# Sink-window attention with a softplus layer on one Trainium2 core: values of the first two chunks as 128 zero-padded columns, and 136 score columns for a batch's first query block

## The chip, the core and the metric

The kernel runs on one core of a Trainium2 chip. The metric is the device time of one launch, in microseconds (us). Before the change three runs took 724.26, 724.29 and 725.24 us, with a median of 724.29 us.

## What is computed

```python
def _attn_ref(q, k, v, n_sink, window):          # 4 batches, 8 heads, 768 positions, 64 per head
    scores = scale * np.matmul(q, k.transpose(0, 1, 3, 2))
    is_sink = pos[None, :] < int(n_sink)         # n_sink = 4
    rel = pos[:, None] - pos[None, :]
    in_window = (rel >= 0) & (rel < int(window)) # window = 128
    scores = np.where(is_sink | in_window, scores, -1000000000.0)
    a = np.exp(scores - np.max(scores, axis=-1, keepdims=True))
    a = a / (np.sum(a, axis=-1, keepdims=True) + 1e-09)
    return np.matmul(a, v)
...
def _moe_ref(x, w_in, w_out):                    # 3072 tokens, 512 -> 2048 -> 512
    h = x @ w_in
    g = np.maximum(h, 0.0) + np.log1p(np.exp(-np.abs(h)))
    return g @ w_out
```

A query sees itself, the 127 positions before it and the first four positions of its batch (the sinks). What the heads give is put side by side, 512 values a token, and goes through the two-layer part.

## The kernel before

The 3072 tokens are cut into 12 chunks of 256 (`CT`), three a batch, and a chunk into two query blocks of 128 (`CH = 2`, index j). Chunks 0, 3, 6 and 9 are the first of their batch (`first`, with `i0 == 0`). Heads are numbered on through all chunks below, so that V11 is `values` of head 3 of chunk 1, T24 is `softmax` of head 0 of chunk 3, and so on.

For a head, `scores` (S) multiplies a query block with 264 columns of keys: the block of keys ahead of it and 8 sink keys (136 columns, `KW`), and then its own block of keys (128 columns). A query sees some keys of both blocks, and for a given place in a block exactly one of two. So `softmax` (T) lays both on each other: `copy_predicated` (L258, on VectorE) puts the scores of the own block over those of the block ahead, where the mask `diag` says so, and a custom reduction (L264) works on the 136 columns that are left, then ScalarE's exp (L265). In a batch's first block (j = 0 of chunks 0, 3, 6 and 9) there is no block ahead, and the layout of the keys puts the own block there a second time.

`normalise` (N) divides; `weights_t` (W) transposes the 128 columns with TensorE (tile `t`), copies them (`th`, and `tl`, the rest that the rounding of `th` leaves) and has GpSimd unfold them into `pt`, with zeros where the other block of keys would stand. `sink_weights` and `sink` (k, K) do the like with the 8 sink columns of four heads at once (`sa`, `ts`, `sk`). `values` (V) is then one product of the sinks' values with `sk` (L342) and two or three products of blocks of values with `pt` (L348), all added in PSUM in the tile `x`, of which there is one. `out` (O) splits `x` into the rounded `xh` and the rest `xl`.

The products have two forms. Chunks 0 and 1 are `exact`: their operands are plain float32, and the profile counts each product as two instructions on TensorE (transposes as one). Later chunks split each number into a float32r high part and a low part and add up products of those; each is one instruction. In `exact` chunks the keys and queries of two heads come together (tiles `k` and `q`, from arrays that the host has laid out, with zeros in q in the half of the other head). The values are loaded for two heads, and a head's 64 columns are its stationary operand: an even head writes partitions 0 to 63 of `x`, an odd one 64 to 127.

The two-layer part of a chunk runs one chunk later: `up` (U, tile `h`, L474), `softplus` and `gate` (F, P, tiles `mt`, `gh`), `residue` (R, `gl`), `down` (D and E, tile `acc`, L511 to L513). Its weights come as 64-bit words in 32 pieces of 512 KB (tiles `wi00r` to `wo71r`, L383), and VectorE, ScalarE and GpSimd turn each into a high and a low float32r part (tiles `upper`, `wt` or `word_ps`, then `wi` or `wo`) while chunks 0 and 1 are worked on.

TensorE and the DMA queue of SyncE run in the order in which the program is written: for chunks 0 and 1 a list of steps by hand (`START`), and from then on two alternating strings of step letters. The other engines' order is set by a scheduler that simulates the program. In `START`, L is `load`, G is `load_v`, w loads a piece of weights, and a, c, d, l are its conversion:

```python
Ctx.START = """
j4 w w w J0 S0 T0 G4 w S1 S2 w N0 L8 T1 T2 S3 w N1 L10 S4 W1 T3 a N2 W0 w T4 a N3 S5 k0 c c K0 a S6
w d c T5 d V0 V1 l N4 l W2 T6 w d O0 a G6 c S7 W3 O1 l N5 N6 T7 z18 V2 a a c N7 d W4 k4 S8 a T8 O2 w V3
...
```

`L10` loads keys and queries into the tiles that S6 and S7 read, so SyncE's queue stands still at it until S7 is done, with the pieces of weights `wi20r` and the rest behind it. The values of chunk 0's heads 4 to 7 and of chunk 1 are loaded at G4, G6, G8, G10, G12 and G14.

Of the kernel before, what the change touches and what calls it, by code (L numbers as in the profile page):

```python
# [11 lines left out]
F32 = mybir.dt.float32  # L12
# [8 lines left out]
B, H, S, D = 4, 8, 768, 64  # L21
DM, DFF = 512, 2048
P = 128
NB = S // P
NS = 8
KW = P + NS
CH = 2
# [10 lines left out]
G = 4  # L38
# [84 lines left out]
class _Attention:  # L123
# [86 lines left out]

    def load_v(self, g):
        c, nc, chunk, lo = self.c, self.c.nc, self.chunk, self.vlo
        tag, bufs = ("kl" if chunk == 0 and g > 1 else "vv", 2) if self.exact else ("vr", 1)
        vr = c.lp.tile([P, 3, 2 * D], F32, tag=tag, name=f"vr{chunk}_{g}", bufs=bufs)
        rows = slice(self.i0 - 1 + lo, self.i0 + 2)
        nc.sync.dma_start(
            vr[:, lo:], c.a["v"][self.b, rows, :, g * 2 * D : (g + 1) * 2 * D].rearrange("n p d -> p n d")
        )
        self.v[g] = vr

    def split_v(self, g):
# [7 lines left out]
        _sub(nc, c.E["vl"], vv[:, lo:, :, 1], src, vv[:, lo:, :, 0])  # L229
        self.v[g] = vv  # L230

    def scores(self, h):
        c, nc = self.c, self.c.nc
        ops = self.heads.pop(h)
        for j in range(CH):
            pool, tag = (c.ps_h, "h") if self.chunk == 0 and h % 2 else (c.ps_s, "s")
            s = pool.tile([P, 2 * P + NS], F32, tag=tag, name=f"s{self.chunk}_{h}_{j}")
            mv = slice(j * KW, j * KW + 2 * P + NS)
            st = slice(KC + j * P, KC + j * P + P)
            if self.exact:  # L240
                q, k = ops
                nc.tensor.matmul(s[:], q[:, j * P : j * P + P], k[:, mv], start=True, stop=True)
            else:
                hi, kl = ops
                nc.tensor.matmul(s[:], hi[:, st], hi[:, mv], start=True, stop=False)  # L245
                nc.tensor.matmul(s[:], hi[:, st], kl[:, mv], start=False, stop=True)  # L246
            self.s[h, j] = s

    def softmax(self, h):
        c, nc, chunk = self.c, self.c.nc, self.chunk  # L250
        g, hh = h // G, h % G
        if hh == 0:
            self.a[g] = c.ap.tile([P, G, CH, KW], F32, tag="a", name=f"a{chunk}_{g}")
            self.rc[g] = c.sp.tile([P, CH, G], F32, tag="rc", name=f"rc{chunk}_{g}")
        sm = c.sp.tile([P, CH], F32, tag="sm", name=f"sm{chunk}_{h}")
        self.sm[h] = sm
        for j in range(CH):
            nc.vector.copy_predicated(self.s[h, j][:, :P], c.diag[:], self.s[h, j][:, KW:])  # L258
        for j in range(CH):
            a = self.a[g][:, hh, j]  # L260
            k = (chunk * H + h) * CH + j
            nm = c.stats[:, k : k + 1]
            m = c.masks[min(self.i0 + j, 2)]
            nc.vector.tensor_tensor_reduce(a, self.s.pop((h, j))[:, :KW], m[:], -SCALE, BIG, ALU.add, ALU.min, nm)  # L264
            nc.scalar.activation(a, a, AF.Exp, bias=nm, scale=-1.0, accum_out=sm[:, j : j + 1])  # L265
# [65 lines left out]
    def values(self, h):  # L331
        c, nc, chunk = self.c, self.c.nc, self.chunk
        pt = self.pt.pop(h)
        r0 = (h % 2) * D
        if self.exact:
            if h % 2 == 0:
                self.xt = c.ps_x.tile([P, 1, CT], F32, tag="x", name=f"x{chunk}_{h}")
            x = self.xt[r0 : r0 + D]
        else:
            x = c.ps_x.tile([P, 2, CT], F32, tag="x", name=f"x{chunk}_{h}")[:]  # L340
        sv = c.vs[self.b, h // G][:, h % G]
        nc.tensor.matmul(x[:, 0], sv, self.sk[h // G], start=True, stop=False, skip_group_check=True)  # L342
        v = self.v[h // 2]
        for n in range(self.vlo, 3):
            w = v[:, n, r0 : r0 + D] if self.exact else v[:, n, h % 2].rearrange("p s d -> p (s d)")
            o = slice(max(0, (n - 1) * P), min(CT, (n + 1) * P))
            m = slice(max(0, (2 * n - 1) * P), min(4 * P, (2 * n + 1) * P))
            nc.tensor.matmul(x[:, :, o], w, pt[:, :, m], start=False, stop=n == 2, skip_group_check=True)  # L348
        self.x[h] = x

    def out(self, h):
# [544 lines left out]
def _blocks(w_in, w_out):  # L896

    w_in = w_in.reshape(4, P, FP, 256).transpose(2, 1, 0, 3).reshape(FP, P, WC)
    w_out = w_out.reshape(FP, 2, P, DM).transpose(0, 2, 1, 3).reshape(FP, P, WC)
    w = np.stack([w_in, w_out], axis=1)  # L900
    return w.view(np.int64) if w.dtype == np.float64 else w


def _layout(q, k, v, n_sink, window, moe_w_in, moe_w_out):
    kT = k.transpose(0, 1, 3, 2)
    kA = np.empty((B, H, D, (NB + 1) * KW), k.dtype)
    for j in range(NB + 1):
        i = max(j - 1, 0)
        kA[..., j * KW : j * KW + P] = kT[..., i * P : i * P + P]
        kA[..., j * KW + P : (j + 1) * KW] = kT[..., :NS]  # L910
    qT = q.transpose(0, 1, 3, 2)
    qk = np.empty((B, NCH, H, D, QK), k.dtype)
    for n in range(NCH):
        qk[:, n, :, :, :KC] = kA[..., n * CH * KW : n * CH * KW + KC]
        qk[:, n, :, :, KC:] = qT[..., n * CT : n * CT + CT]
    first = qk[0, : Ctx.EXACT].reshape(Ctx.EXACT, H // 2, 2, D, QK)
    k0 = np.ascontiguousarray(first[..., :KC]).reshape(Ctx.EXACT, H // 2, P, KC)
    q0 = np.zeros((Ctx.EXACT, H // 2, 2, D, 2, CT), k.dtype)
    for e in range(2):
# [21 lines left out]
```

## Time and profile before

| | |
|---|---|
| median of three runs | 724.29 us |
| the profiled execution's own time | 724.42 us |
| its span, first to last instruction | 722.7 us |
| TensorE (PE) busy, granted clock | 701.4 us, 0.998 |
| VectorE (DVE), ScalarE (ACT), GpSimd (POOL) busy | 581.5, 452.5, 373.8 us |
| bytes moved by DMA | 63.21 MB |

The execution's time is 1.7 us over its span, and 0.13 us over the median of the runs. A busy time counts an instruction from start to end, and TensorE's instructions overlap: what a product costs there is the distance from its start to the next one's start. PEld is TensorE's loading of the stationary operand. "issue" in the chain of waits is time for which the profile shows no cause.

### The profile page before, as it was taken

The page shows a single profiled execution, that of the slowest core. Times are in us where ns is not written, and L with a number is a line of the kernel's source. Part 1 is how long each engine was busy: PE and PEld are TensorE (multiplying, and loading weights), DVE is VectorE, ACT ScalarE, POOL GpSimd, SP SyncE. Part 2 cuts the span into 40 slices and gives each one's busy share as a digit, 9 for nine tenths or more (in the row PEclk, how much of TensorE's full clock was granted, in tenths as well). Part 3 has the DMA queues.
Part 4 walks back from the last instruction along what each step waited for, and adds up shares of the span by engine and source line. Part 5 has one row for each costly group of instructions (what it writes and reads, how often), then busy time and mean ns, then how long its engine had stood idle before and what let it go on. Part 6 is the DMA issues. An engine that isn't in the chain of part 4 may idle for free.

```text
span 722.7 us, 13866 instructions
## 1 busy us (share of the span) xinstructions
PE 701.4 (97%) x4535; PEld 624.5 (86%) x4535; DVE 581.5 (80%) x1693; ACT 452.5 (63%) x1104; POOL 373.8 (52%) x676
## 2 busy tenths in 40 slices
PE   7889999999999999999999999999999999999996
PEld 5577789988998898998999899898888898999995
DVE  6899988888987987888888987988888887855332
ACT  4679847666666666766666666666665766643431
POOL 5867485655455564655544564564555465452000
PEclk9999999999999999999999999999999999999999
DMA  9887713221221411321321322222221312100000
GB/s 309 289 303 223 197 49 90 58 72 58 81 66 37 122 49 50 109 64 46 101 68 49 98 59 67 80 75 64 75 74 52 96 51 77 60 12 1 30 2 34
DMA packets 40875, 63.21 MB, mean 87 GB/s; under 512 B 4634, under 2 KB 22362, under 8 KB 40794
## 3 DMA queue, kind: packets, MB, share of 16 engines
q1 hardware_dynamic: 40506, 61.97, 28.0%
q8 instruction: 38, 0.62, 0.4%
q14 instruction: 43, 0.35, 0.2%
q10 hardware_dynamic: 288, 0.26, 0.1%
HBM read 55.93 MB, written 6.29 MB: 86 GB/s over the span
## 4 chain that ended last, share of the span: by engine, by line
PE 69%; DVE 14%; ACT 8%; issue 4%; POOL 3%; DMA 2%; SPq 0%; ACTq 0%; POOLq 0%; DVEq 0%
PE h L474 28%; PE acc L513 9%; PE acc L511 9%; PE acc L512 9%; PE x L348 5%; PE t L312 2%; PE s L245 2%; PE s L246 2%; DVE gl L56 2%; POOL pt L323 2%; ACT a L265 1%; PE x L342 1%; DVE kl L56 1%; ACT mt L482 1%; DVE mt L489 1%
## 5 line engine op out<-in xcount | busy, mean ns | idle before, releaser
L474 PE MATMUL h<-xh,wi 128*128 128x256 f32 x1536 | 253.8, 288 | 0.0
L474 PEld LDWEIGHTS h<-xh,wi 128*128 128x128 f32 x1536 | 211.2, 191 | 1.6 <-issue 0.5
L279 POOL TENSOR_SCALAR a<-a,rc 128x128 f32<-128x128 f32 x178 | 69.3, 402 | 188.9 <-DVE rc L272 150.5
L474 PE MATMUL h<-xl,wi 128*128 128x256 f32 x768 | 154.6, 283 | 0.0
L511 PE MATMUL acc<-wo,gh 128*128 128x512 f32 x384 | 151.8, 395 | 0.0
L513 PE MATMUL acc<-wo,gl 128*128 128x512 f32 x384 | 151.0, 393 | 0.7 <-DVE gl L56 0.7
L512 PE MATMUL acc<-wo,gh 128*128 128x512 f32 x384 | 150.7, 393 | 0.0
L474 PEld LDWEIGHTS h<-xl,wi 128*128 128x128 f32 x768 | 119.7, 192 | 0.0
L489 DVE SCALAR_TENSOR_TENSOR mt<-h,mt 128x512 f32<-128x512 f32 x96 | 66.0, 687 | 63.3 <-ACT mt L483 54.5
L481 ACT ACTIVATE mt<-h 128x512 f32<-128x512 f32 x96 | 57.1, 595 | 93.8 <-PE h L474 93.8
L265 ACT ACTIVATE a<-a,stats 128x136 f32<-128x136 f32 x192 | 76.4, 399 | 58.2 <-DVE stats L264 57.7
L513 PEld LDWEIGHTS acc<-wo,gl 128*128 128x128 f32 x384 | 72.2, 188 | 17.5 <-DVE gl L56 1.1
L511 PEld LDWEIGHTS acc<-wo,gh 128*128 128x128 f32 x384 | 72.3, 188 | 12.8 <-issue 0.3
L56 DVE TENSOR_TENSOR gl<-mt,gh 128x512 fp32r<-128x512 f32 x96 | 79.9, 832 | 0.3
L512 PEld LDWEIGHTS acc<-wo,gh 128*128 128x128 f32 x384 | 72.3, 188 | 8.9
L323 POOL TENSOR_SCALAR_AFFINE_SELECT pt<-tl 128x256 fp32r<-128x256 f32 x80 | 60.1, 751 | 29.6 <-DVE tl L56 28.9
L323 POOL TENSOR_SCALAR_AFFINE_SELECT pt<-th 128x256 fp32r<-128x256 f32 (+1 forms) x96 | 44.2, 460 | 36.1 <-ACT th L48 33.1
L482 ACT ACTIVATE mt<-mt 128x512 f32<-128x512 f32 x96 | 60.7, 633 | 3.1
L483 ACT ACTIVATE mt<-mt 128x512 f32<-128x512 f32 x96 | 60.7, 632 | 3.0
L48 ACT CAST qkh<-qk 128x656 fp32r<-128x656 f32 x80 | 59.5, 744 | 2.5 <-DMA qk<-qk 2.5
L56 DVE TENSOR_TENSOR kl<-qk,qkh 128x400 fp32r<-128x400 f32 x80 | 52.7, 658 | 2.5
L56 DVE TENSOR_TENSOR tl<-t,th 128x256 f32<-128x256 f32 x80 | 33.2, 415 | 24.5 <-ACT th L48 24.1
(185 smaller groups left out, 1245.2 us busy)
## 6 DMA issues: line engine op xcount, KB each, us to landing
qk<-qk SPq DMA_DIRECT2D x160, 164.0 KB, 3.0
vr<-v SPq DMA_DIRECT2D x32, 192.0 KB, 2.7
out<-o SPq DMA_DIRECT2D x24, 256.0 KB, 2.3
vr<-v SPq DMA_DIRECT2D x16, 128.0 KB, 2.4
q<-q SPq DMA_DIRECT2D x7, 256.0 KB, 4.6
k<-k SPq DMA_DIRECT2D x8, 200.0 KB, 4.6
wi00r<-w SPq DMA_DIRECT2D x1, 511.8 KB, 5.3
wi01r<-w SPq DMA_DIRECT2D x1, 511.8 KB
```

Source lines behind the costliest of these rows:

```text
L48: nc.scalar.copy(out, in_)
L56: (nc.vector if eng == "V" else nc.gpsimd).tensor_tensor(out, a, b, ALU.subtract)
L265: nc.scalar.activation(a, a, AF.Exp, bias=nm, scale=-1.0, accum_out=sm[:, j : j + 1])
L279: (nc.vector if eng == "V" else nc.gpsimd).tensor_scalar(a, a, rc[:, j : j + 1], 0.0, ALU.mult, ALU.add)
L323: nc.gpsimd.affine_select(pt[:, e, :, 1], src[:], [[0, CH], [1, P]], ALU.is_ge, 0.0, base=0, channel_multiplier=-1)
L474: nc.tensor.matmul(h[:, j], wt, x, start=k == 0, stop=k >= len(prods) - 2, skip_group_check=True)
L482: nc.scalar.activation(t[:], t[:], AF.Exp, scale=-1.0)
L483: nc.scalar.activation(t[:], t[:], AF.Ln, bias=1.0)
L489: nc.vector.scalar_tensor_tensor(t[:], h[:], 0.0, t[:], ALU.max, ALU.add)
L511: nc.tensor.matmul(acc[:], gh[:, j, q], wh, start=f == 0, stop=False, skip_group_check=True)
L512: nc.tensor.matmul(acc[:], gh[:, j, q], wl, start=False, stop=False, skip_group_check=True)
L513: nc.tensor.matmul(acc[:], gl[:, j, q], wh, start=False, stop=f == 2 * FP - 1, skip_group_check=True)
```

## The change

In chunks 0 and 1 the values come from a new array `v0`, in which each head's 64 columns stand in a block of 128, an even head's in the first half and an odd one's in the second, zeros beside them. All products of a pair of heads now write the 128 partitions of `x`, and one product with the sinks' values of both heads takes the place of two. In a batch's first query block (`lone`) the scores have the 136 columns of the keys ahead and the sinks alone (where the own block stands too), and `copy_predicated` is left out. The values of chunk 0's heads 4 to 7 are put in the tiles `mt` instead of `kl`.

```diff
     def load_v(self, g):
-        tag, bufs = ("kl" if chunk == 0 and g > 1 else "vv", 2) if self.exact else ("vr", 1)
-        vr = c.lp.tile([P, 3, 2 * D], F32, tag=tag, name=f"vr{chunk}_{g}", bufs=bufs)
+        if self.exact:
+            pool, tag = (c.mp, "mt") if chunk == 0 and g > 1 else (c.lp, "vv")
+            vz = pool.tile([P, 3 - lo, 2, P], F32, tag=tag, name=f"vz{chunk}_{g}", bufs=2)
+            nc.sync.dma_start(vz[:], c.a["v0"][chunk, g, :, lo:])
+            self.v[g] = vz
+            return
+        vr = c.lp.tile([P, 3, 2 * D], F32, tag="vr", name=f"vr{chunk}_{g}", bufs=1)
...
+    def lone(self, j):
+        return self.first and j == 0
...
     def scores(self, h):
+            w = KW if self.lone(j) else 2 * P + NS
+            mv = slice(j * KW, j * KW + w)
-                nc.tensor.matmul(s[:], q[:, j * P : j * P + P], k[:, mv], start=True, stop=True)
+                nc.tensor.matmul(s[:, :w], q[:, j * P : j * P + P], k[:, mv], start=True, stop=True)
-                nc.tensor.matmul(s[:], hi[:, st], hi[:, mv], start=True, stop=False)
-                nc.tensor.matmul(s[:], hi[:, st], kl[:, mv], start=False, stop=True)
+                nc.tensor.matmul(s[:, :w], hi[:, st], hi[:, mv], start=True, stop=False)
+                nc.tensor.matmul(s[:, :w], hi[:, st], kl[:, mv], start=False, stop=True)
...
     def softmax(self, h):
         for j in range(CH):
+            if self.lone(j):
+                continue
             nc.vector.copy_predicated(self.s[h, j][:, :P], c.diag[:], self.s[h, j][:, KW:])
...
     def values(self, h):
-            x = self.xt[r0 : r0 + D]
+            x = self.xt[:]
+            g = h % G // 2 * 2
+            sv = c.vs[self.b, h // G][:, g : g + 2].rearrange("p h d -> p (h d)")
...
-        nc.tensor.matmul(x[:, 0], sv, self.sk[h // G], start=True, stop=False, skip_group_check=True)
+        if not (self.exact and odd):
+            nc.tensor.matmul(x[:, 0], sv, self.sk[h // G], start=True, stop=False, skip_group_check=True)
         for n in range(self.vlo, 3):
-            w = v[:, n, r0 : r0 + D] if self.exact else v[:, n, h % 2].rearrange("p s d -> p (s d)")
+            w = v[:, n - self.vlo, h % 2] if self.exact else v[:, n, h % 2].rearrange("p s d -> p (s d)")
...
+    v0 = np.zeros((Ctx.EXACT, H // 2, P, 3, 2, 2, D), v.dtype)   # in _layout, on the host
```

On all engines the program's order stays as it was, but for the instructions that go. Names below carry counters behind them, which differ between the two programs. On TensorE, V13 (an odd head of chunk 1) stands between the transposes of head 14 and a step of `up`. Before:

```order
L312 MATMUL t_6_1263<-ident,a_1_674 128x128 x2
L342 MATMUL x_4_1189<-sk_1_1135,vsf_188 64x256
L348 MATMUL x_4_1189<-pt_5_1199,vr_2_823 64x128
L348 MATMUL x_4_1189<-pt_5_1199,vr_2_823 64x256
L348 MATMUL x_4_1189<-pt_5_1199,vr_2_823 64x128
L474 MATMUL h_6_1285<-xh_379,wi_1040 128x256 x4
```

After:

```order
L324 MATMUL t_6_1249<-ident,a_1_662 128x128 x2
L364 MATMUL x_4_1175<-pt_5_1185,vz_2_810 128x128
L364 MATMUL x_4_1175<-pt_5_1185,vz_2_810 128x256
L364 MATMUL x_4_1175<-pt_5_1185,vz_2_810 128x128
L490 MATMUL h_6_1270<-xh_371,wi_1027 128x256 x4
```

The product with the sinks' values is gone, and the three that stay write 128 rows instead of 64; nothing has moved around them.

On VectorE, in chunk 0, this is T3 with what follows it (`ISA` is the custom reduction and the reading of its result). Before:

```order
L272 RECIPROCAL rc_0_205<-sm_1_235 128x2
L258 COPY_PREDICATED s_3_0_249<-diag,s_3_0_249 128x128
L258 COPY_PREDICATED s_3_1_251<-diag,s_3_1_251 128x128
L264 ISA a_0_204,stats<-s_3_0_249,mask_159 128x136
L264 ISA stats 128x1
L264 ISA a_0_204,stats<-s_3_1_251,mask_160 128x136
L264 ISA stats 128x1
L271 TENSOR_SCALAR sm_2_242<-sm_2_242 128x2
```

After:

```order
L284 RECIPROCAL rc_0_205<-sm_1_234 128x2
L270 COPY_PREDICATED s_3_1_248<-diag,s_3_1_248 128x128
L276 ISA a_0_204,stats<-s_3_0_246,mask_159 128x136
L276 ISA stats 128x1
L276 ISA a_0_204,stats<-s_3_1_248,mask_160 128x136
L276 ISA stats 128x1
L283 TENSOR_SCALAR sm_2_240<-sm_2_240 128x2
```

One copy of the two is gone, and the reductions follow as before. On SyncE's queue the loads keep their places; those of values have 512 or 768 numbers a partition now, where they had 256 or 384.

More of the change, by code (lines that the diff above doesn't have):

```diff
@@ L237, in scores @@
             s = pool.tile([P, 2 * P + NS], F32, tag=tag, name=f"s{self.chunk}_{h}_{j}")
-            mv = slice(j * KW, j * KW + 2 * P + NS)
+            w = KW if self.lone(j) else 2 * P + NS
+            mv = slice(j * KW, j * KW + w)
             st = slice(KC + j * P, KC + j * P + P)
@@ L333, in values @@
         pt = self.pt.pop(h)
-        r0 = (h % 2) * D
+        odd = h % 2 == 1
         if self.exact:
-            if h % 2 == 0:
+            if not odd:
                 self.xt = c.ps_x.tile([P, 1, CT], F32, tag="x", name=f"x{chunk}_{h}")
-            x = self.xt[r0 : r0 + D]
+            x = self.xt[:]
+            g = h % G // 2 * 2
+            sv = c.vs[self.b, h // G][:, g : g + 2].rearrange("p h d -> p (h d)")
         else:
             x = c.ps_x.tile([P, 2, CT], F32, tag="x", name=f"x{chunk}_{h}")[:]
-        sv = c.vs[self.b, h // G][:, h % G]
-        nc.tensor.matmul(x[:, 0], sv, self.sk[h // G], start=True, stop=False, skip_group_check=True)
+            sv = c.vs[self.b, h // G][:, h % G]
+        if not (self.exact and odd):
+            nc.tensor.matmul(x[:, 0], sv, self.sk[h // G], start=True, stop=False, skip_group_check=True)
         v = self.v[h // 2]
         for n in range(self.vlo, 3):
-            w = v[:, n, r0 : r0 + D] if self.exact else v[:, n, h % 2].rearrange("p s d -> p (s d)")
+            w = v[:, n - self.vlo, h % 2] if self.exact else v[:, n, h % 2].rearrange("p s d -> p (s d)")
             o = slice(max(0, (n - 1) * P), min(CT, (n + 1) * P))
             m = slice(max(0, (2 * n - 1) * P), min(4 * P, (2 * n + 1) * P))
-            nc.tensor.matmul(x[:, :, o], w, pt[:, :, m], start=False, stop=n == 2, skip_group_check=True)
+            last = n == 2 and (odd or not self.exact)
+            nc.tensor.matmul(x[:, :, o], w, pt[:, :, m], start=False, stop=last, skip_group_check=True)
         self.x[h] = x
@@ L920, in _layout @@
         q0[:, :, e, :, e] = first[:, :, e, :, KC:]
+    vb = v.transpose(0, 2, 1, 3).reshape(B, NB, P, H // 2, 2, D)
+    v0 = np.zeros((Ctx.EXACT, H // 2, P, 3, 2, 2, D), v.dtype)
+    for n in range(Ctx.EXACT):
+        for k in range(3):
+            i = n * CH - 1 + k
+            for e in range(2 * (i >= 0)):
+                v0[n, :, :, k, e, e] = vb[0, i, :, :, e].transpose(1, 0, 2)
     return {
@@ L923, in _layout @@
         "k0": k0,
+        "v0": v0.reshape(Ctx.EXACT, H // 2, P, 3, 2, P),
         "q0": q0.reshape(Ctx.EXACT, H // 2, P, 2, CT),
```

## The prediction

> **What bounds the kernel now.** First the page's shares, the slices of the span and the chain that ended last:
>
> ```profile
> span 722.7 us, 13866 instructions
> PE 701.4 (97%) x4535; PEld 624.5 (86%) x4535; DVE 581.5 (80%) x1693; ACT 452.5 (63%) x1104; POOL 373.8 (52%) x676
> PE   7889999999999999999999999999999999999996
> DVE  6899988888987987888888987988888887855332
> PE 69%; DVE 14%; ACT 8%; issue 4%; POOL 3%; DMA 2%; SPq 0%; ACTq 0%; POOLq 0%; DVEq 0%
> ```
>
> TensorE is full from the fifth slice on (a slice is 18 us), and the chain runs mainly over it. Ahead of that it isn't full, and VectorE is at its fullest there. So the stages need separate readings. The waits of TensorE from 80 us to the end, and those of VectorE from 36 to 95 us (total, times, longest):
>
> ```profile
> PE x L348 <- POOL pt L326: 2.9, 8, 0.5
> ```
>
> ```profile
> DVE qkh L56 <- ACT qkh L48: 0.4, 1, 0.4
> DVE xl L56 <- ACT xh L48: 0.3, 1, 0.3
> ```
>
> From 80 us on TensorE waits 2.9 us in 640, at the first products of some heads, and once more, 0.7 us, for `gl` at 79.58. What it is spared there shortens the program one for one. Between 36 and 95 us VectorE stands still for 0.7 us only, since it converts weights: there a faster TensorE gains next to nothing.
>
> The front is a chain over all engines, here in pieces:
>
> ```profile
> 7.59 0.40 DVE s L258 x2
> ...
> 13.28 0.40 DVE s L258 x2
> ...
> 17.00 0.58 PE x L342 x2
> ...
> 19.08 0.89 PE s L242 x4
> ...
> 20.38 0.43 SPq L191
> ...
> 20.85 7.38 DMA wi20r<-w
> ```
>
> Five pairs of L258 stand in it (T0 to T4; the first and the last are shown). Then come S6, V0, V1, S7 on TensorE, and the end of S7 lets SyncE's queue load the next keys and `wi20r`, which the chain waits for until 28.2. In that time the DMA engines had nothing to do (busy share and GB/s at the row's end):
>
> ```profile
> 18.00:19.00 1.00, 1.00 (x11) 0.67 (x7) 1.00 (x8) 0.26 (x1) 1.00 (x1) 1.00 0.81 326
> 19.00:20.00 1.00, 1.00 (x6) 0.65 (x6) 0.96 (x5) 1.00 (x5) 0.60 (x3) 1.00 0.06 25
> 20.00:21.00 1.00, 1.00 (x10) 1.00 (x10) 1.00 (x6) 0.65 (x4) 1.00 (x2) 1.00 0.04 8
> ```
>
> **The price of a product.** The durations of the page overlap; distances from start to start are wanted. In the row of S7, 4 instructions in 0.89 us, a float32 instruction of 264 columns takes 0.22 us, by its columns 0.215 for 256, 0.11 for 128 and 0.115 for 136. A group of `values` in the timeline (V11):
>
> ```profile
> 71.01 0.29 PE L245 MATMUL s<-qkh 128*128 128x264 f32 x1
> 71.13 0.28 PE L246 MATMUL s<-kl,qkh 128*128 128x264 f32 x1
> 71.34 0.65 PE L342 MATMUL x<-sk,vsf 128*64 128x256 f32 x2
> 71.82 1.03 PE L348 MATMUL x<-pt,vr 128*64 128x128 f32 x6
> 72.79 0.74 PE L474 MATMUL h<-xh,wi 128*128 128x256 f32 x4
> 73.37 0.40 PE L474 MATMUL h<-xl,wi 128*128 128x256 f32 x2
> ```
>
> From the start of L246 to that of the second L474 row are 2.24 us. L246 has 0.12 of it (71.01 to 71.13), and four products of L474 have 0.48, by this row:
>
> ```profile
> 140.32 2.89 PE h L474 x24
> ```
>
> So the group costs 1.64. Its instructions by their columns make 2 x 0.215 (sinks) + 4 x 0.11 + 2 x 0.215 = 1.30. The other 0.34 is lost in front of the first 128*64 instruction and behind the last one, where the stationary operand changes between 64 and 128 columns (0.21 instead of 0.12 before L342, 0.58 instead of 0.48 for the four L474). All products having 128 columns, I let go of the 0.34 for every group, and of another 0.43 in an odd head, whose sink product goes: 0.77.
>
> Against giving up the 64 columns speaks the Trainium skill's page "TensorEngine Tiling (Array Packing)", section "Theoretical Speedup": with a small dimension of up to 64 the array holds two tiles that work side by side, up to twice as fast. By that rule the pair of heads loses its overlap. The trace has it in the two places only where an even and an odd head stand back to back, V0 with V1 and V6 with V7:
>
> ```profile
> 16.93 0.65 PE L342 MATMUL x<-sk,vsf 128*64 128x256 f32 x2
> 17.41 0.38 PE L348 MATMUL x<-pt,vr 128*64 128x256 f32 x1
> 17.42 0.43 PE L342 MATMUL x<-sk,vsf 128*64 128x256 f32 x1
> ...
> 18.64 0.43 PE L312 MATMUL t<-ident,a 128*128 128x128 f32 x2
> ```
>
> V1's first instruction starts 0.01 us behind one of V0. The pair takes 1.71 us up to the transposes; afterwards it takes 2 x 0.215 + 4 x 0.215 + 4 x 0.11 = 1.73, so nothing is won and nothing lost. V11 above, alone, shows no such overlap, and 12 of the 16 heads stand alone.
>
> **The change part by part.**
>
> 1. Front, to `wi20r`. One copy of each of five pairs: 5 x 0.20 = 1.0 us. S6 and S7, two instructions each from 0.22 to 0.115: 0.43. V0 and V1: nothing. S7 could end 1.4 us earlier, near 18.6. But the three loads of values that stand ahead of it grow by 128 KB each:
>
> ```profile
> vr<-v SPq DMA_DIRECT2D x16, 128.0 KB, 2.4
> ```
>
> At 326 GB/s that is 1.2 us, so that the DMA engines come free near 20.2 instead of 19.0. The loads that went out at 20.0 to 20.9 thus gain between 0 (if the added bytes delay them fully) and 1.4; I take 0.8, as the hole of 1.9 us takes in most of both. The copies of T5 to T7 and the other shorter scores lie beside the wait for `wi20r`: nothing.
>
> 2. From 28 to 60 us the chain has V4 on it:
>
> ```profile
> 30.84 0.57 PE x L342 x2
> ```
>
> This even head gives 0.34 at most; I take 0.3. What follows is ScalarE's, VectorE's and GpSimd's work, unchanged.
>
> 3. From 60 to 80 us V10 and V11 spare TensorE 0.34 + 0.77, but it then waits for VectorE's `gl` at 79.58, and VectorE can make up no more than the 0.4 us that it stood waiting for `qkh`. Bounds 0 and 1.1, I take 0.3.
>
> 4. From 80 us TensorE sets the pace. Groups on the chain:
>
> ```profile
> 81.26 0.58 PE x L342 x2
> ...
> 101.93 0.58 PE x L342 x2
> ```
>
> These are the first and the last of four, V12 to V15: 0.34 + 0.77 + 0.34 + 0.77 = 2.2 us. Lower bound 1.8, if loading 128 columns instead of 64 shows beside the 128-column products (0.01 or 0.02 on each).
>
> 5. Later copies, 8 in each of chunks 3, 6 and 9. VectorE is no bound, but one of the waits of L348 has a copy pair in its chain:
>
> ```profile
> 164.96 0.41 DVE s L258 x2
> ...
> 172.77 0.44 POOL pt L326
> ...
> 173.25 0.61 PE x L348 x2
> ```
>
> One copy less there brings `pt` 0.2 us sooner. Three chunks: between 0 and 0.6; I take 0.4.
>
> 6. The short float32r scores, 2 x 8 x 3 = 48, on TensorE where it is full:
>
> ```profile
> L245 PE MATMUL s<-qkh 128*128 128x264 f32 x160 | 44.2, 295 | 0.0
> ```
>
> Today's distance is 0.123 (71.01 to 71.13 and its like). No row shows a float32r product under 256 columns. The nearest row with a new 128-column stationary operand for 128 moving columns is the transposes:
>
> ```profile
> 95.32 0.22 PE t L312 x2
> ```
>
> 0.11 each. Longer ones, L474 with 256 columns at 0.12 and this with 512 at 0.23, lie on a line that would come to 0.07 at 136, if nothing but columns and a small fixed part counted:
>
> ```profile
> 94.60 0.23 PE acc L513
> ```
>
> I take 0.115, near the transposes: they too bring 128 new stationary columns for every 128 or so moving ones, and lie far above that line's 0.065 for 128. It makes 48 x 0.008 = 0.4 us; 0.3 reaches the end, since the waits of step 5 eat the gain of a head or two. Ends: 2.5 gained (0.07), or a loss, for which see the rivals.
>
> 7. The later, larger loads of values: 128 KB more once and 192 KB four times, 0.9 MB, 2.7 us at 326 GB/s, between 22 and 75 us. They come ahead of weights that VectorE is behind in converting: no wait of VectorE or TensorE for a load stands in the rows above after 36 us. Nothing; without this cover at most 2.7.
>
> Sum: 0.8 + 0.3 + 0.3 + 2.2 + 0.4 + 0.3 = 4.3 us. Against the profiled execution's 724.42 that is 720.1, and the median of the runs is 0.13 under that execution, which I leave out.
>
> **The rivals.**
>
> The other side: a short float32r product runs at float32's rate. A float32 product of 136 columns is 2 x 0.115 = 0.23, so each of 48 loses 0.107 where the forecast gains 0.008: 5.1 us on TensorE's path in chunks 3, 6 and 9. With the 4.0 of the other steps that gives 725.5, slower than before; it decides from 0.21 us a product on. Against it: the products stay single instructions, and 256, 264 and 512 columns (0.12, 0.123, 0.23) fit one line. For it: no shorter one was ever seen here. Chance 8%.
>
> The columns alone count: 0.07 each, 2.5 instead of 0.3, 717.9. Against it stand the transposes' 0.11. 8%. The skill's "TensorE: Matmul & The Clock Gate", section "LDWEIGHTS (loading the stationary operand)", gives a load of P columns P / 1.2 ns, which is 107 ns for 128 and would forbid 0.07; the transposes agree with it, and no run so far shows it for float32r.
>
> The front stays where it is, `wi20r` and VectorE absorbing steps 1, 2, 3 and 5: 2.2 + 0.3 are left, 721.9. 17%.
>
> The added bytes aren't covered: step 1 gives nothing and 2.0 of the 2.7 us of step 7 show: 724.42 - 4.3 + 0.8 + 2.0 = 722.9. Against it the hole of 1.9 us and VectorE's rows. 6%.
>
> **How the numbers follow.** Forecast 58%, the others as given, 3% for what I don't see. Runs agree within about 0.2%, or 1.4 us. Faster by more: forecast, front and columns, and half of the bytes, 86%. Within: the other half, most of the slow rate, 10%. Slower 4%. The range 718.3 to 722.9 holds the forecast with steps 1 and 3 at their ends, the front and the bytes, and leaves out the short products' two extremes.
>
> **What would show it.** Right: L258 has 160 instructions, and the `values` groups of chunk 1 cost 0.87 or 1.30 us with 0.12 ahead of them and 0.12 per L474 behind; the last wait for `gl` near 79.6 comes 1 to 2 us sooner, and TensorE is 3 to 4 us ahead at the place that is now 105 us; 136-column products stand 0.11 to 0.12 apart. Wrong: 0.23 there (slow rate), 0.07 (columns), `wi20r` landing at 28.2 or later (bytes), or the change between 64 and 128 columns' 0.34 turning out to belong to float32 against float32r, and staying.

## The result, and the profile after

| | before | after |
|---|---|---|
| median of 5 runs each | 724.29 us (724.02 to 725.24) | 720.62 us (719.83 to 721.12) |
| ratio, 95% interval | | 0.9946 (0.9935 to 0.9958) |
| the profiled execution: own time, span | 724.42, 722.7 us | 719.83, 718.1 us |

The kernel is faster by 3.7 us, 0.5%, against a forecast of 720.1. The profiled execution after the change is the fastest of its five, so the traces show 4.6 us of span. The page's span, shares and chain shares:

```profile
span 718.1 us, 13796 instructions
PE 694.7 (97%) x4519; PEld 624.9 (87%) x4519; DVE 575.1 (80%) x1661; ACT 451.8 (63%) x1104; POOL 374.3 (52%) x676
PE 72%; DVE 9%; ACT 9%; issue 4%; POOL 3%; DMA 2%; SPq 0%; POOLq 0%; ACTq 0%; DVEq 0%
```

TensorE lost 16 instructions and 6.7 us of busy time, VectorE 32 copies and 6.4 us, and VectorE's share of the chain has gone from 14% to 9%, TensorE's from 69% to 72%. The waits of TensorE from 78 us to the end, and that of VectorE from 35 to 94 us:

```profile
PE x L364 <- POOL pt L338: 2.7, 6, 0.5
PE acc L529 <- DVE gl L56: 0.6, 1, 0.6
```

```profile
DVE xl L56 <- ACT xh L48: 0.3, 1, 0.3
```

As before, TensorE waits for `gl` once near 79 us, then only for `pt`, at six heads instead of eight, and VectorE still has no slack up to 94 us.

Where the time went is read as a lead: the median by which the rows of `up` and `down` (L490, L527 to L529) start earlier than the same rows before. It is taken near 46, 79, 107, 196, 365, 534 and 670 us; the columns between are differences, and chunk 3's is that from 107 to 196 us, chunk 6's from there to 365, chunk 9's to 534. The kernels of the experiments stand in the same table. Each row is one trace against the one trace of the kernel before, so what that trace alone has (a slow transfer, say) shows in every row.

| kernel | lead at 46 us | 46 to 79 | 79 to 107 | chunk 3 | chunk 6 | chunk 9 | lead near 670 us |
|---|---|---|---|---|---|---|---|
| after | 1.02 | 0.13 | 1.63 | 0.48 | 0.36 | 0.40 | 4.11 |
| `changed_again`, the same program | 1.25 | 0.12 | 1.62 | 0.45 | 0.37 | 0.43 | 4.37 |
| `values_alone` | 0.20 | 0.12 | 1.64 | -0.01 | -0.09 | -0.04 | 1.82 |
| `scores_alone` | 1.10 | -0.02 | 0.02 | 0.46 | -0.01 | 0.39 | 2.04 |
| `cols264_nocopy` | 0.74 | 0.10 | 1.65 | 0.39 | -0.14 | 0.33 | 3.17 |
| `sink_pair_64` | -0.09 | 0.43 | 0.84 | 0.46 | 0.41 | 0.49 | 2.63 |
| `cols200` | 0.41 | 0.12 | 1.66 | 0.51 | 0.47 | 0.49 | 3.75 |
| `vz1_later` | 1.45 | 0.12 | 1.62 | 0.02 | 0.39 | 0.04 | 3.72 |
| `vz01_later` | 0.83 | 0.10 | 1.64 | 0.00 | 0.00 | 0.03 | 2.68 |
| `v13_behind_u6` | 0.26 | 0.12 | 2.04 | 0.52 | 0.41 | 0.41 | 3.87 |
| `warm` | 1.02 | 0.11 | 1.64 | 0.46 | 0.40 | 0.40 | 4.15 |
| `warm_v13` | 0.85 | 0.13 | 2.01 | 0.12 | 0.39 | 0.41 | 4.00 |
| `warm_v13_vz1` | 1.10 | 0.12 | 2.00 | -0.37 | -0.09 | -0.21 | 2.63 |

Behind 670 us another 0.5 us of the 4.6 comes from the last store alone: VectorE's last copy ended 5.9 us ahead of the span's end before, 5.4 after. The change does not touch that.

**The groups.** V11 in the timeline after the change:

```profile
70.06 0.28 PE L256 MATMUL s<-kl,qkh 128*128 128x264 f32 x1
70.18 1.04 PE L364 MATMUL x<-pt,vz 128*128 128x128 f32 x6
70.97 0.72 PE L490 MATMUL h<-xh,wi 128*128 128x256 f32 x4
71.53 0.40 PE L490 MATMUL h<-xl,wi 128*128 128x256 f32 x2
```

From L256 to the second L490 row are 1.47 us instead of 2.24. Less 0.12 and 0.48 the group costs 0.87, as forecast: 0.77 is gone, the sink product and the 0.34 both. V12, V14 and V15 cost 1.30, 1.30 and 0.89 by the same reading (before 1.59, 1.64 and 1.64).

**The front.** The chain up to 36 us no longer runs over S7 and `wi20r`, but from the landing of `wi01r` over the conversion of weights:

```profile
7.49 6.71 DMA wi01r<-w
14.30 0.53 DVE upper L50
...
17.25 0.69 DVE wt L434
...
20.20 1.26 POOL wi L56
```

`wi20r` went out 0.34 us earlier than before (20.85), not 0.8, but nothing waits for it any more: ScalarE converts it at 26.53 instead of 28.32, so it took at most 6.0 us where it had taken 7.38.

```profile
20.51 0.43 SPq L399 DMA_DIRECT2D wi20r<-w  x1
```

The hole in the DMA work from 19 us on has shrunk (busy share 0.06 and 0.04 before):

```profile
19.00:20.00 1.00, 0.80 (x6) 0.39 (x5) 0.97 (x7) 0.80 (x3) 0.60 (x3) 1.00 0.66 258
20.00:21.00 1.00, 1.00 (x11) 1.00 (x10) 1.00 (x5) 0.85 (x5) 1.00 (x2) 1.00 0.55 148
```

The lead at 46 us is a sum of several moves. They are read from the start of T0's first copy and from the starts of transposes (L324, and L308 for those of the sinks), against the same ones before:

| place, us before the change | after | `changed_again` | `values_alone` | `scores_alone` | `cols264_nocopy` |
|---|---|---|---|---|---|
| T0's first copy, 7.5 | -0.06 | -0.07 | -0.59 | 0.23 | -0.52 |
| transposes, 12.3 | 0.37 | 0.53 | -0.70 | 0.86 | 0.03 |
| sink transposes, 15.7 | 0.01 | 0.18 | -0.70 | 0.50 | -0.26 |
| sink transposes, 28.9 | 0.15 | 0.31 | -0.73 | 0.64 | -0.14 |
| transposes, 30.4 | 0.75 | 0.91 | -0.13 | 1.24 | 0.46 |
| behind V4, 33.0 | 1.09 | 1.25 | 0.20 | 1.24 | 0.79 |
| sink transposes, 43.0 | 1.69 | 1.90 | 0.86 | 1.81 | 1.39 |
| behind V8's wait, 46.9 | 0.97 | 1.19 | 0.15 | 1.10 | 0.68 |

The first row is the landing of a small load (`words`), which comes at 5.6 to 6.4 us. `values_alone` and `cols264_nocopy` have the same loads as the changed kernel up to there, so their half microsecond of lag is a difference between executions, and it stays in all their rows. All five gain 0.60 between 28.9 and 30.4, where TensorE waits for ScalarE's `sk` before the change, since `sk` comes behind the conversion of the late `wi20r`:

```profile
30.40 0.44 PE L312 MATMUL t<-ident,a 128*128 128x128 f32 x2 [1.11 <-ACT sk L48]
```

After the change:

```profile
29.65 0.44 PE L324 MATMUL t<-ident,a 128*128 128x128 f32 x2 [0.51 <-DVE xl L56]
```

V4 gives 0.34 where the values are padded, and nothing in `scores_alone`. All five gain another 0.6 up to 43.0 and lose 0.7 at V8, which waits for `sk` 0.62 us before and 1.37 after:

```profile
45.45 0.65 PE L342 MATMUL x<-sk,vsf 128*64 128x256 f32 x2 [0.62 <-ACT sk L48]
```

```profile
44.51 0.70 PE L357 MATMUL x<-sk,vsf 128*128 128x256 f32 x2 [1.37 <-ACT sk L48]
```

**The short products.** A head of chunk 3, TensorE's own rows and then its loads of stationary operands (PEld):

```profile
167.96 0.23 PE L255 MATMUL s<-qkh 128*128 128x136 f32 x1
168.02 0.27 PE L256 MATMUL s<-kl,qkh 128*128 128x136 f32 x1
168.13 0.34 PE L255 MATMUL s<-qkh 128*128 128x264 f32 x1
168.31 0.29 PE L256 MATMUL s<-kl,qkh 128*128 128x264 f32 x1
168.43 0.40 PE L527 MATMUL acc<-wo,gh 128*128 128x512 f32 x1
```

```profile
167.84 0.19 PEld L255 LDWEIGHTS s<-qkh 128*128 128x128 f32 x1
167.96 0.19 PEld L256 LDWEIGHTS s<-kl,qkh 128*128 128x128 f32 x1
168.07 0.19 PEld L255 LDWEIGHTS s<-qkh 128*128 128x128 f32 x1
168.18 0.19 PEld L256 LDWEIGHTS s<-kl,qkh 128*128 128x128 f32 x1
168.31 0.19 PEld L527 LDWEIGHTS acc<-wo,gh 128*128 128x128 f32 x1
```

The first short product seems to cost 0.06 (167.96 to 168.02), but a later one of 264 columns then takes 0.18 instead of 0.12. The loads tell it plainly: they follow each other by 0.11 where a short product runs, and by 0.12 otherwise. The sum over the four products is 0.468 us, where it was 0.494: 0.025 a head, 0.6 for 24 heads.

### The profile page after: what moved, and what is told of

Read it like the earlier page. It is cut to its first block, busy times and chain, and to the rows that moved or that the text cites. A ratio compares the mean times of both kernels' runs of the same rounds, so it can differ in the third digit from the quotient of the medians.

```text
span 718.1 us, 13796 instructions
## 1 busy us (share of the span) xinstructions
PE 694.7 (97%) x4519; PEld 624.9 (87%) x4519; DVE 575.1 (80%) x1661; ACT 451.8 (63%) x1104; POOL 374.3 (52%) x676
## 4 chain that ended last, share of the span: by engine, by line
PE 72%; DVE 9%; ACT 9%; issue 4%; POOL 3%; DMA 2%; SPq 0%; POOLq 0%; ACTq 0%; DVEq 0%
PE h L490 30%; PE acc L527 10%; PE acc L529 10%; PE acc L528 10%; PE x L364 5%; PE t L324 2%; PE s L255 2%; PE s L256 2%; POOL pt L335 2%; ACT a L277 2%; ACT mt L498 1%; ACT mt L497 1%; POOL pt L338 1%; ACT mt L499 1%; ACT upper L48 1%
## 5 line engine op out<-in xcount | busy, mean ns | idle before, releaser
L490 PE MATMUL h<-xh,wi 128*128 128x256 f32 x1536 | 253.5, 287 | 0.0
L490 PEld LDWEIGHTS h<-xh,wi 128*128 128x128 f32 x1536 | 211.0, 191 | 0.9
L490 PE MATMUL h<-xl,wi 128*128 128x256 f32 x768 | 154.6, 283 | 0.0
L527 PE MATMUL acc<-wo,gh 128*128 128x512 f32 x384 | 151.9, 396 | 0.0
L529 PE MATMUL acc<-wo,gl 128*128 128x512 f32 x384 | 150.7, 393 | 0.6 <-DVE gl L56 0.6
L490 PEld LDWEIGHTS h<-xl,wi 128*128 128x128 f32 x768 | 119.5, 191 | 0.0
L529 PEld LDWEIGHTS acc<-wo,gl 128*128 128x128 f32 x384 | 72.1, 188 | 17.8 <-DVE gl L56 1.1
L527 PEld LDWEIGHTS acc<-wo,gh 128*128 128x128 f32 x384 | 72.1, 188 | 12.6
```

What stands on the lines that cost most here:

```text
L490: nc.tensor.matmul(h[:, j], wt, x, start=k == 0, stop=k >= len(prods) - 2, skip_group_check=True)
L527: nc.tensor.matmul(acc[:], gh[:, j, q], wh, start=f == 0, stop=False, skip_group_check=True)
L529: nc.tensor.matmul(acc[:], gl[:, j, q], wh, start=False, stop=f == 2 * FP - 1, skip_group_check=True)
```

## The experiments

The kernels ran in three groups of four, each group beside runs of the kernel before. Its median was 723.99, 723.81 and 724.99 us in the three, so times are compared by their ratios to it.

### The parts alone

`values_alone`: every score product and copy as before, values as in the changed kernel.

```diff
     def lone(self, j):
-        return self.first and j == 0
+        return False
```

> The padded values with one sink product a pair, as in the changed kernel, but every score product keeps 264 columns and its copy. Theory A (the gain of the changed kernel came in three separate places: about 1.1 us up to 75 us from the missing copies and short scores, 1.65 us at V12 to V15 from the values, 1.3 us in chunks 3, 6 and 9 from the scores): only the second place is left, and the larger loads delay the first weights by about 1 us without a shorter front to set against it. 724.3 - 1.65 + 0 to 0.6: 722.9 (722.4 to 723.5); TensorE 1 to 1.7 us ahead at 105 us, nothing gained between 130 and 530 us. Rival B (the front's 1.1 us came from the values as well, V4, V10 and V11): 721.6, TensorE 1 us ahead already at 75 us.

Measured: 722.25 us, ratio 0.9977 (0.9968 to 0.9986). The lead is 0.20 at 46 us, then 1.64 at V12 to V15, and nothing in chunks 3, 6 and 9. Theory A holds in the last two places. For the front the lead alone doesn't decide, since 0.5 us of it is the late small load; but rival B's 721.6 lies outside the interval, which is 722.0 to 723.3 against 724.29.

`scores_alone`: the kernel before with `lone`, the short products and the missing copy.

> 136 columns without the copy, as in the changed kernel; the values are loaded and multiplied as before. Theory A: the front gains 1.1 to 2.0 us (five copies and shorter S6 and S7, and no added bytes ahead of the weights), nothing at V12 to V15, 1.3 us in chunks 3, 6 and 9: 721.5 (721.0 to 722.2). Rival B (front from the values): only the 1.3 us of chunks 3, 6 and 9, 723.0. Rival C (VectorE's pace up to 80 us takes the front's gain back, whatever comes earlier): 722.6 to 723.0 with the waits for gl near 79.6 us longer.

Measured: 722.09 us, ratio 0.9975 (0.9964 to 0.9986). 1.10 of lead at 46 us, nothing at V12 to V15, then chunks 3 and 9. Chunk 6 gave nothing, which theory A did not foresee (for this see the races below). By its ratio the time is 722.5 against 724.29, above theory A's range and near rival C's, so A rests on the leads here; the longer wait for `gl` of rival C isn't there (0.7 us, as before). Without added bytes the lead at 28.9 us is 0.64 instead of 0.15 and 0.31, but 0.3 of this stands at T0's first copy already: those bytes cost 0.5 there at most. The two parts alone bring 0.23% and 0.25%, both together 0.54%: within the intervals they add up.

### The copy against the columns

`cols264_nocopy`:

```diff
-            w = KW if self.lone(j) else 2 * P + NS
+            w = 2 * P + NS
```

> The changed kernel, but the lone block's score product runs over 264 columns again (its copy stays out). Theory A (a 136-column product costs 0.11 because the next 128-column stationary operand takes that long to load, so a head's four products take 0.468 instead of 0.494): 24 heads give back 24 x 0.025 = 0.6 us, S6 and S7 0 to 0.4; 721.3 (720.9 to 721.8). The copies' share in chunks 3, 6 and 9, about 0.25 us a chunk, stays. Rival (the starts in the trace, 0.064 behind the first short one, are the price: 0.071 saved a pair, and the copies gave nothing there): 24 x 0.071 = 1.7, 722.3, with three waits for pt in each of these chunks again.

Measured: 720.79 us, ratio 0.9952 (0.9939 to 0.9966). Its profiled run is the slowest of its five, 721.8. Chunks 3 and 9 still gain 0.39 and 0.33 without the shorter columns, against 0.36 to 0.48 with them. So the copies carry these chunks, about 0.36 each; of the columns' 0.2 a chunk some 0.05 arrives, less than such chunks differ from trace to trace (0.36 to 0.52). The rival (1.7 us from columns, none from copies) falls. At 46 us the lead is 0.3 to 0.5 smaller, but 0.5 was missing at T0's first copy, ahead of S6 and S7: what these two save doesn't show.

`cols200`: 200 columns for the lone block in chunks 3, 6 and 9.

```diff
-            w = KW if self.lone(j) else 2 * P + NS
+            w = 200 if self.lone(j) and not self.exact else KW if self.lone(j) else 2 * P + NS
```

> The changed kernel with 200 instead of 136 columns in the lone block's products of chunks 3, 6 and 9 (the result doesn't use the added ones). Theory A (the load of the next 128-column stationary operand, 0.108 to 0.111, sets the pace): the four products of a head still take 0.468 to 0.473, since 200 columns by the line of 256 and 512 (0.12, 0.23) take 0.096. Rival (columns count, on a line from 0.468 at 136 to 0.494 at 264): 0.481. Time as the changed kernel's, 720.6.

Measured in one run: 720.3 us, and the head that answers to the one above:

```profile
168.54 0.26 PE L255 MATMUL s<-qkh 128*128 128x200 f32 x1
168.63 0.27 PE L256 MATMUL s<-kl,qkh 128*128 128x200 f32 x1
168.74 0.30 PE L255 MATMUL s<-qkh 128*128 128x264 f32 x1
168.88 0.28 PE L256 MATMUL s<-kl,qkh 128*128 128x264 f32 x1
169.00 0.39 PE L527 MATMUL acc<-wo,gh 128*128 128x512 f32 x1
```

0.464 us, no more than with 136 columns. The loads set the pace, and cutting 200 to 136 buys nothing. It agrees with the Trainium skill's "TensorE: Matmul & The Clock Gate", section "LDWEIGHTS (loading the stationary operand)", whose P / 1.2 ns makes 107 ns for 128 columns; the loads behind a short product stand 0.108 to 0.112 us apart here.

### What the 0.34 was

`sink_pair_64`: one sink product a pair, but values loaded and multiplied with 64 columns as before.

```diff
+            y = x[r0 : r0 + D] if self.exact else x
-            nc.tensor.matmul(x[:, :, o], w, ...)
+            nc.tensor.matmul(y[:, :, o], w, ...)      # w = v[:, n, r0 : r0 + D]
```

> The changed kernel, but values loaded and multiplied with 64 columns as before (no zeros, no added bytes); the one sink product a pair stays. Theory A (0.34 us a group is the change between 64 and 128 stationary columns, 0.43 an odd head's sink product): V11 costs 0.87 + 0.34 = 1.21 instead of 0.87, V12, V14 and V15 0.34 more each, V13 nothing since it waits for pt: +0.7 to 1.0 there; the front gets back 0.3 to 1.0 since the first weights land 1 us sooner. 720.9 (720.3 to 721.7). Rival (the 0.34 came with the second sink product or with float32 against float32r): groups as in the changed kernel, 0.87 and 1.30, and 719.6 to 720.3.

Measured: 721.33 us, ratio 0.9967 (0.9956 to 0.9978). V11 there:

```profile
71.01 0.28 PE L251 MATMUL s<-kl,qkh 128*128 128x264 f32 x1
71.22 1.08 PE L360 MATMUL x<-pt,vr 128*64 128x128 f32 x6
72.23 0.74 PE L486 MATMUL h<-xh,wi 128*128 128x256 f32 x4
72.81 0.40 PE L486 MATMUL h<-xl,wi 128*128 128x256 f32 x2
```

1.80 from the first to the last row instead of 1.47: the 0.33 is back, without a second sink product and with float32 and float32r mixed just as in the changed kernel. So it belongs to the change between 64 and 128 stationary columns, and not to narrow products as such: inside the group they follow each other by 0.11 and 0.215 as the wide ones do, and the time is lost around its first instruction (0.21 and 0.16 instead of 0.12 and 0.11) and behind its last one (0.20 and 0.22 instead of 0.11 and 0.12). From 79 to 107 us this kernel gains 0.84, as 0.43 for each of V13 and V15 would give. Its front fell behind for another reason (the clock, below), so the forecast of a better front stays untested.

### V13

In the changed kernel V13 is the group of step 4 that gave less than its share (TensorE's rows, with the idle time ahead of V13):

```profile
85.73 0.38 PE L324 MATMUL t<-ident,a 128*128 128x128 f32 x2
86.38 1.14 PE L364 MATMUL x<-pt,vz 128*128 128x128 f32 x6 [0.27 <-POOL pt L338]
```

`v13_behind_u6` moves it:

```diff
-V13 O13 U6 D4 E4
+U6 V13 O13 D4 E4
```

> The changed kernel with V13 and O13 moved behind U6 on TensorE; no other engine's order changes. Theory F (step 4 gave 1.65 instead of 2.2 because V13 got through its 0.77 sooner only to wait 0.5 us for its pt): the wait is gone, TensorE is 0.4 to 0.5 us further ahead at 105 us than in the changed kernel, and the end comes as much sooner: 720.1. Rival G (pt and gl come at VectorE's and GpSimd's pace, so that the wait comes back at V14, V15 or a later head): 720.6.

Measured: 720.14 us (719.33 to 720.28), ratio 0.9948 (0.9934 to 0.9962). V13 no longer waits:

```profile
89.37 0.40 PE L490 MATMUL h<-xl,wi 128*128 128x256 f32 x2
89.61 1.04 PE L364 MATMUL x<-pt,vz 128*128 128x128 f32 x6
```

The gain from 79 to 107 us is 2.04 instead of 1.63, and 2.01 and 2.00 in the two other kernels with this edit. Theory F holds there. Whether it reaches the end is not settled: here it does, but in `warm_v13` chunk 3 gave only 0.12. TensorE's load for a sink product waits there at 135.09 us:

```profile
PEld x L357 <- DVE sk L56: 0.4, 1, 0.4
```

Neither the changed kernel nor `v13_behind_u6` has this wait, so rival G's wait did come back in that trace, at another input. The ratio can't be told from the changed kernel's.

### The loads in front

`vz1_later` loads the second pair's values behind three pieces of weights, `vz01_later` the first pair's too, behind two.

```diff
-        att[0].load_v(1)
...
-j4 w w w J0 S0 T0
+j4 w w w G2 J0 S0 T0        (vz01_later: j4 w w G0 w G2 J0)
```

> The changed kernel with one load moved: the padded values of the second pair (256 KB) go out behind the first three loads of weights instead of ahead of them; no other engine's order changes. Theory D (in the changed kernel the front's chain runs from the landing of wi01r, 14.2 us, over VectorE's conversion behind it, and the added bytes hold that landing up): wi01r lands about 0.8 us sooner (256 KB at 326 GB/s), and the end comes 0.3 to 0.8 us sooner: 720.0. Rival E (VectorE's own queue of work sets the pace from 14 to 75 us, whenever the weights land): within 0.2 us of the changed kernel at 75 us, 720.6.

> The same with the first pair's values too: they go out behind wi01r. Theory D: wi01r lands 1.6 us sooner than in the changed kernel, near 12.6, and the end comes 0.6 to 1.3 us sooner: 719.6. Rival E: 720.6, TensorE at 75 us within 0.2 us of the changed kernel. A loss is possible if the first pair's values land behind 16.6 us, where V0 wants them: 721.

Measured: 720.25 and 720.15 us, ratios 0.9951 (0.9937 to 0.9964) and 0.9950 (0.9936 to 0.9964). The chain of waits of `vz1_later` has `wi01r` land at 13.5 us:

```profile
6.81 6.71 DMA wi01r<-w
```

In the changed kernel it is 14.2. The chain goes on over S7 and SyncE's queue there, and the lead at 46 us is 1.45, 0.2 to 0.4 more than without the edit: D holds in part. But chunks 3 and 9 then gave nothing. In `vz01_later` VectorE no longer waits for the piece (it converts it at 13.28 us, behind other work), yet the lead at 46 us is only 0.83, and none of the three chunks gave anything: its forecast of 719.6 fails. No faster version comes of it.

### The races and the clock

In nearly all kernels with short scores or without the copies, each of chunks 3, 6 and 9 gives 0.33 to 0.52 or else nothing, and one pair of rows near 175 us (and like ones near 345 and 513) tells which. VectorE's subtraction `gl` and GpSimd's `pt` start within 0.03 us of each other. After the change:

```profile
175.10 1.21 DVE L56 TENSOR_TENSOR gl<-mt,gh 128x512 fp32r<-128x512 f32 x1
```

```profile
175.12 0.40 POOL L335 TENSOR_SCALAR_AFFINE_SELECT pt<-th 128x256 fp32r<-128x256 f32 x1
```

And in `vz1_later`:

```profile
174.71 0.68 DVE L56 TENSOR_TENSOR gl<-mt,gh 128x512 fp32r<-128x512 f32 x1
```

```profile
174.73 0.93 POOL L335 TENSOR_SCALAR_AFFINE_SELECT pt<-th 128x256 fp32r<-128x256 f32 x1
```

One of the two takes 0.53 us longer: `gl` 1.21 instead of 0.68, or `pt` 0.93 instead of 0.40. The recorded starts don't tell which: `gl`'s stands 0.01 to 0.03 us ahead in all these rows, whichever is lengthened, so what decides it stays open. In the latter case V waits for `pt` longer (its loads 0.9 us between 160 and 190 us in `vz1_later`, 0.4 after the change), and the chunk's gain is gone. The long `pt` stands at these places in nine chunks of five traces, and in no other: `scores_alone` 6, `cols264_nocopy` 6, `vz1_later` 3 and 9, `vz01_later` all three, `warm_v13_vz1` 3 and 6. These are just the table's chunks of 0.04 or less, but for `values_alone`, which has nothing to gain there, and chunk 9 of `warm_v13_vz1`, lost at 473.78 us, where the load for a sink product waits 0.70 us for `sk`. `warm_v13_vz1` has such a wait in chunk 3 too, 0.46 us, beside the long `pt`. The Trainium skill's "Trainium Architecture — The Big Picture", section "What this means for kernel authors", says that these two engines contend for a shared pair of ports by an exclusive lock; the rows agree in that one of the two is held up, but no run here shows that the ports are the reason.

Some profiled runs show a second thing. After the change S5 ends earlier, but the sink transposes behind it wait for `sa` as long as before, so that TensorE's gap grows from 1.01 us (before) to 1.50:

```profile
15.71 0.38 PE L308 MATMUL ts<-ident,sa 128*32 128x128 f32 x2 [1.50 <-DVE sa L296]
```

In three of six traces with a gap of 1.50 to 1.55 us, the granted clock then falls (the third number from a row's end; `v13_behind_u6`):

```profile
16.00:18.00 2.00, 2.00 (x7) 1.71 (x7) 1.76 (x4) 1.13 (x3) 0.73 (x1) 0.50 1.02 400
```

The three are `sink_pair_64`, `cols200` and this one. Their leads at 46 us are -0.09, 0.41 and 0.26, at least 0.6 below the 1.02 to 1.25 of the other three. In eight traces with a gap of 1.30 or less it never falls. The record of the granted clock tells the three from the other three. In all fourteen traces the times between its changes are whole multiples of 3.41 us, and each fall lasts 3.41 us. Cut at this beat, the stretch ahead of each fall has TensorE busy for a share of 0.41 to 0.44; no stretch of the other eleven traces between 10 and 20 us has less than 0.56. `cols200`, the stretch of the gap and the next one:

```profile
12.07:15.48 3.41, 1.51 (x8) 0.84 (x7) 2.39 (x13) 2.52 (x11) 2.50 (x7) 1.00 1.04 416
15.48:18.89 3.41, 3.33 (x10) 2.79 (x11) 3.06 (x5) 1.49 (x4) 1.26 (x1) 0.50 1.04 402
```

`scores_alone` has the same gap in one stretch and keeps the clock; TensorE is busy all the rest of it there (1.90 us, a share of 0.56):

```profile
12.70:16.11 3.41, 1.90 (x12) 1.26 (x12) 2.89 (x9) 2.87 (x13) 2.40 (x6) 1.00 1.02 377
```

The first record of the full clock stands at 5.2 to 7.6 us, so the gap falls on another part of the beat in each run. The share alone is not the whole rule: at the end of the span a stretch of 0.44 in `sink_pair_64` and one of 0.46 in `scores_alone` have no fall behind them. The last group was to take the gap away and to combine what had helped:

```diff
-N3 S5 k0 c c K0
+N3 S5 z8 k0 c c K0          (warm: eight idle products behind S5)
```

> The changed kernel itself, on the same chip as the next three: 720.6 (719.8 to 721.2). What can differ between its runs, by the traces so far: whether the granted clock falls to 0.5 for 3 us near 16 us (theory H: TensorE's gap ahead of the sink transposes, 1.50 us in the changed kernel, is at the edge; price 0.8 us), and whether pt or VectorE's subtraction goes first at 175 us and its like (price 0.4 to 0.5 a chunk).

> The changed kernel with eight idle products of 256 columns (0.96 us, into a bank nothing reads) behind S5, in TensorE's gap of 1.5 us; no other order changes. Theory H (the gap lets the granted clock fall to 0.5 in some runs, 0.8 us each): the gap ahead of the sink transposes is 0.5 to 0.7 us, the clock stays at 1.00 from 14 to 20 us, and the median falls by 0 to 0.5 us: 720.3, with no run over 721. Rival I (the fall has nothing to do with the gap, or VectorE takes its price back): the same median and spread as the changed kernel; a loss of up to 0.3 if the products delay the sink transposes.

> The eight idle products and V13 with O13 behind U6. Theories F and H together: V13's wait of 0.5 us is gone and no run has the fallen clock: 719.8 (719.3 to 720.3), TensorE 3.2 us or more ahead of the kernel before at 105 us. Rival G or I: 720.4.

> The last kernel, and the second pair's values loaded behind the first three loads of weights. Theory D in part (wi01r lands 0.7 us sooner, and TensorE was 0.4 us further ahead from 45 to 165 us with that load alone): 719.4. Rival J (what is won ahead of 165 us is taken back in chunks 3, 6 and 9, where pt or VectorE's subtraction goes first by 0.02 us): 719.8, the same as the last kernel.

Measured, beside 724.99 for the kernel before:

| kernel | median (range) | ratio (95%) |
|---|---|---|
| `changed_again` | 722.04 (719.84 to 722.25) | 0.9956 (0.9943 to 0.9970) |
| `warm` | 721.68 (720.38 to 722.49) | 0.9953 (0.9939 to 0.9966) |
| `warm_v13` | 721.12 (720.14 to 721.58) | 0.9944 (0.9931 to 0.9958) |
| `warm_v13_vz1` | 721.48 (720.37 to 722.26) | 0.9946 (0.9932 to 0.9959) |

All four medians lie 1.3 to 2.1 us above what was expected; the kernel before is slower in this group too, by 0.7 us, and by the ratios the changed kernel gains 0.44% here where it had gained 0.54%, with intervals that overlap. Its trace is the fastest of its five again, by 1.9 us, so no trace shows what the slower executions lose. The gap is 0.59 us in the last three and no clock fell in their traces, but neither did it in `changed_again`'s. The spread of `warm` is hardly narrower (2.1 us, against 2.4) and three of its runs lie above 721, where theory H had none: that the clock sets the changed kernel's spread is not shown. `warm_v13` has the lowest ratio, though its interval holds the changed kernel's too. Rival J fits `warm_v13_vz1`: ahead by 3.22 us at 107, it lost 0.6 again by 670.

## Why the prediction was right

The time is 0.5 us from the forecast. The parts are the right ones and three of them work by the forecast mechanism (the groups of values, the later copies, the short products). But the sizes of two steps miss by as much in opposite directions, and the front's came about in another way: that the sum fits is in part luck. Step by step, with the leads:

1. **Front (0.8) and 2. V4 (0.3).** 1.02 and 1.25 in two traces of the program, for 1.1 together. That fits by luck. The missing copies bring TensorE forward at first, by 0.37 and 0.53 at 12.3 us, but the sink transposes at 15.7 us wait for VectorE's `sa`, behind the conversion of `wi01r`, and have 0.01 and 0.18 left. At 28.9 us the lead is 0.15 and 0.31, where the step had 0.8 from an earlier end of S7: that path was wrong. The added bytes delay `wi01r`, by 0.7 us where one load is moved away; what they cost is 0.2 to 0.4 us by `vz1_later`, at most 0.5 by `scores_alone`, and `vz01_later` gains nothing by moving more. The next 0.60 comes from `wi20r`, no longer waited for, but not because it goes out sooner: that is 0.34 us, while its transfer is at least 1.3 us shorter, and `values_alone`, which sends it 0.66 later than before, gains the same 0.60. Why the transfer was slow in the trace of the kernel before, no run shows. V4 brings its 0.34 as forecast. What the 0.6 behind it belongs to stays open; the wait for `sk` at V8, of which the prediction says nothing, takes it back.
3. **V10 and V11 (0.3).** V11's group got 0.77 shorter as forecast, and the lead grows to 1.81 behind it, but 0.1 is left of it at 79 us. The wait that takes it is not the one for `gl`, which hardly changes (0.67 to 0.64 us), but the one of the sink transposes ahead of it, 0.52 us before and 1.25 after:

```profile
75.55 0.38 PE L308 MATMUL ts<-ident,sa 128*32 128x128 f32 x2 [1.25 <-DVE sa L296]
```

VectorE's pace is the bound, as the step said, but at another of its outputs. Inside the bounds, near the lower one.

4. **V12 to V15 (2.2).** Mis-sized: 1.63. V12, V14 and V15 are as short as forecast to 0.05 us, but V13 waits for `pt` and gives 0.21 of its 0.77, which is all that is missing. Moving V13 brought 0.4 of the missing 0.57. The step added up groups without asking whether a head's next input was due. TensorE is 2.8 and 3.0 us ahead at 107 us, not 3 to 4 as the prediction's signs had it.
5. **Copies in chunks 3, 6 and 9 (0.4, at most 0.6).** Mis-sized the other way: 0.36 a chunk, 1.1 us. I counted the one copy pair next to the wait. The chain of waits of the kernel before holds three between 143 and 173 us, that one (164.96) and two ahead of it:

```profile
151.99 0.40 DVE s L258 x2
...
158.28 0.40 DVE s L258 x2
```

Each sheds 0.2, so that up to 0.6 a chunk was there. The waits at the loads (PEld) in chunk 3 before and after show it:

```profile
PEld x L348 <- POOL pt L326: 0.8, 2, 0.6
```

```profile
PEld x L364 <- POOL pt L338: 0.4, 1, 0.4
```

6. **Short float32r products (0.4, of which 0.3 reaches the end).** In TensorE's time 0.6: the pace is 0.11, not 0.115. At the end about 0.2, by a difference of 0.05 a chunk that single traces hardly resolve; that the wait for `pt` eats the rest, as the step had said of a head or two, is not shown.
7. **Later loads (0).** No new wait for a load in TensorE's or VectorE's rows after 36 us; `values_alone` loses nothing anywhere.

Against the forecast's 4.3 stand 1.02 + 0.13 + 1.63 + about 1.1 + 0.2 = 4.1. Steps 3 and 4 fell short by 0.7, step 5 made that up, by luck.

The rivals: the slow rate falls (loads 0.11 apart, no 0.23), and so does that of columns alone, though the first start-to-start distance of 0.06 looks like its 0.07. The front did not stay at 46 us, though up to 28.9 us it nearly did; the added bytes cost 0.5 at most by these traces, where that rival had 2.8, and `wi20r` did not land at 28.2 or later. The 0.34 did not stay with float32 against float32r.

## What to carry to other kernels

The price of a short TensorE instruction is read from the sum over its whole group or from the loads of stationary operands, never from the distance to the next start. Before adding up what shorter groups save, look for the next wait behind each one: what is saved ahead of it is lost, while work taken off the chain that feeds the wait counts as often as it stands in that chain. Where a narrow stationary operand stands alone among wide ones, weigh what its narrowness saves against the price of the change, here 0.34 us a group. And before two traces are compared at a place far down, compare them at the first step, where executions with the same loads can differ already, here by half a microsecond.

## What the runs showed of the hardware

- Changing between 64 and 128 stationary columns costs 0.33 to 0.34 us a group, around the first and behind the last narrow instruction; between them narrow products keep the pace of wide ones, 0.11 for 128 float32 columns.
- A float32r product of 136 or 200 columns is paced by the load of the next 128 stationary columns, 0.108 to 0.112 us: four products of a head take 0.468 and 0.464 us.
- When a VectorE subtraction of 128x512 and a GpSimd select of 128x256 start within 0.03 us of each other, one of the two takes 0.53 us longer. Which one moves a chunk by 0.4 us, and the recorded starts don't tell it.
- The granted clock changes on a beat of 3.41 us. Between 10 and 20 us it fell to 0.5 for one beat where TensorE had been busy for 0.41 to 0.44 of the beat ahead (three traces), and stayed at 1.00 where that was 0.56 or more (eleven). A gap of 1.5 us was among both.
